# Two more landing buffers for weights, a mask added by matmul, and another order of first loads, in a fused attention and MoE kernel

## The chip, the cores and the metric

One core of one Trainium2 chip runs the whole program. The metric is the device time of one execution in microseconds (us); lower is better. The core has TensorE (PE in the rows; PEld is its weight load), VectorE (DVE), ScalarE (ACT) and GpSimd (POOL); SyncE (SP) issues most of the DMAs.

## The reference

Attention in windows, then two MoE-like blocks, all in fp32:

```python
scores = q @ k.T / sqrt(64)       # 4 batches, 8 heads, 576 positions
# heads 0-3: the last 32 positions; heads 4-7: every 4th of the last 128
attn = softmax(where(mask, scores, -1e9)); x = attn @ v        # 2304 x 512
y = ((x @ w1) * (x @ w2)) @ w3 @ w_out                         # 512 -> 1024 -> 512
z = (silu(y @ w_gate) * (y @ w_val)) @ moe2_w_out              # 512 -> 1536 -> 512
```

## The kernel before

**Numbers.** Every weight and activation that a large matmul uses is kept as a high and a low part, and each product is three matmuls into one bank (`mm3`, lines 182 to 187). The 37 weight blocks of 1 MB hold 64-bit words and are turned into parts on the chip (`convert_weights`, lines 152 to 173): a DMA lands the block in a `raw` buffer, ScalarE rescales the upper words (L166), VectorE shifts the lower words right by 29 (L167) and joins the two (L168), ScalarE copies the high part (L172), GpSimd subtracts for the low part (L173). Then the buffer is given back and the next load is issued (`done_with`, `load_block`). There are three `raw` buffers while blocks 0 to 19 pass, then two.

**Stages.** First, w3 and w_out of the first MoE block are multiplied into one matrix W in 16 steps s (lines 431 to 451). Steps 0 to 7 need one new block each among 0 to 7 (a pair of blocks per two steps from 2 on), steps 8 to 15 one per two steps (blocks 8 to 11). In between stand the units of attention of batch 0: its four pairs of heads, each in `scores`, `transposes` and `values`; they end in `x0`, the tokens of chunk 0. Blocks 12 to 19 are w1 and w2. Then `stage1` takes 5 chunks of 512 tokens (the last has 256) through w1, w2 and W, with the attention of batches 1 to 3 inside chunks 0 to 2; it goes through DRAM (`x1d`) into the next chunk's `x`. The second MoE block follows (lines 513 to 537).

**Scores** (lines 280 to 317): 5 or 4 matmuls per group fill a bank; VectorE scales and adds the mask (L300) and takes the row maximum (L303); ScalarE does 9 exponentials a pair (L305); VectorE adds 1e-9 and inverts (L308, L309); GpSimd multiplies (L310). The transposes (L323) go back through ScalarE (L325), the values are L338.

**Order.** Each engine runs its instructions in the order of its queue. A scheduler fixes that order when the program is built, from a model of durations.

Of the kernel before, what the change touches and what calls it, by code (L numbers as in the profile page):

```python
# [70 lines left out]
def moe_chain_kernel(tc, q_in, k_in, v_in, w_in, mask_in, out):  # L71
# [8 lines left out]
    with static as st, other as ot, psum as pp, dram as dp:  # L80

        wslot = [st.tile([P, 2, 2, 512], F32R, name=f"w{i}") for i in range(12)]
        xb = [st.tile([P, 2, KT, CMAX], F32R, name=f"x{i}") for i in range(2)]
# [154 lines left out]
        att1_pool = tc.tile_pool(name="att1", bufs=1)  # L238
        att2_pool = tc.tile_pool(name="att2", bufs=1, side="right")
        with att1_pool as a1, att2_pool as a2:  # L240
# [8 lines left out]
            sc = [a2.tile([P, NBLK, KW], F32, name=f"s{i}") for i in range(2)]  # L249
            pt = a2.tile([P, NBLK, P], F32, name="pt")  # L250
            mask = a2.tile([P, NBLK, KW], F32, name="mask")
            ident = a2.tile([P, P], F32, name="ident")
            sm = [a2.tile([P, 3, NBLK], F32, name=f"sm{i}") for i in range(2)]
# [26 lines left out]
            def scores(i, g):  # L280
# [11 lines left out]
                v = ps[:, :nb * KW].rearrange("p (n k) -> p n k", k=KW)  # L292
                if i % NPAIR >= NPAIR // 2:
                    parts = [(b0, b1, mask[:, b0:b1])]
                else:
                    parts = [(0, 1, mask[:, 0:1])] if g == 0 else []
                    lo = max(b0, 1)
                    parts.append((lo, b1, mask[:, 1:2].to_broadcast([P, b1 - lo, KW])))
                for lo, hi, mk in parts:
                    nc.vector.scalar_tensor_tensor(  # L300
# [303 lines left out]
```

## Time and profile before

| what | us |
|---|---|
| median of 3 runs (907.78 to 911.71) | 909.82 |
| the profiled execution, its own time | 909.69 |
| its span, first to last instruction | 907.5 |
| TensorE busy | 881.4 (97%) |
| VectorE, ScalarE, GpSimd busy | 336.0, 312.3, 132.0 |

TensorE's busy time counts pipelined matmuls from start to a modelled end, so 97% does not mean that it runs at its peak. The granted clock (PEclk) is a share of 2.4 GHz; 0.5 is the lower level, 1.2 GHz.

### The profile page before, as it was taken

The page shows a single profiled execution, that of the slowest core. Times are in us where ns is not written, and L with a number is a line of the kernel's source. Part 1 is how long each engine was busy: PE and PEld are TensorE (multiplying, and loading weights), DVE is VectorE, ACT ScalarE, POOL GpSimd, SP SyncE. Part 2 cuts the span into 40 slices and gives each one's busy share as a digit, 9 for nine tenths or more (in the row PEclk, how much of TensorE's full clock was granted, in tenths as well). Part 3 has the DMA queues.
Part 4 walks back from the last instruction along what each step waited for, and adds up shares of the span by engine and source line. Part 5 has one row for each costly group of instructions (what it writes and reads, how often), then busy time and mean ns, then how long its engine had stood idle before and what let it go on. Part 6 is the DMA issues. An engine that isn't in the chain of part 4 may idle for free.

```text
span 907.5 us, 11771 instructions
## 1 busy us (share of the span) xinstructions
PE 881.4 (97%) x4850; PEld 737.6 (81%) x4850; DVE 336.0 (37%) x487; ACT 312.3 (34%) x682; POOL 132.0 (15%) x83
## 2 busy tenths in 40 slices
PE   8889899989999999999999999999999999999998
PEld 5667688868888878889988888888888888888998
DVE  5887952333324213344766313111221112111221
ACT  4966743343525423343555212111221112111111
POOL 4656531000100100321343000000000000000000
PEclk8989899999999999999999999999999999999999
DMA  9786622332224113333555302000010001000100
GB/s 296 253 275 237 211 61 61 93 126 88 77 91 155 33 46 116 122 119 139 208 178 173 106 1 70 1 0 1 1 47 1 0 1 47 1 0 1 47 1 24
DMA packets 45909, 79.58 MB, mean 88 GB/s; under 512 B 3232, under 2 KB 29472, under 8 KB 41120
## 3 DMA queue, kind: packets, MB, share of 16 engines
q1 hardware_dynamic: 40096, 69.39, 23.5%
q10 hardware_dynamic: 5760, 9.44, 2.8%
q8 instruction: 38, 0.62, 0.3%
q14 instruction: 15, 0.12, 0.0%
HBM read 65.72 MB, written 13.11 MB: 87 GB/s over the span
## 4 chain that ended last, share of the span: by engine, by line
PE 83%; DVE 6%; DMA 4%; ACT 3%; issue 2%; POOL 1%; SPq 0%; DVEq 0%; POOLq 0%; ACTq 0%
PE bk L185 26%; PE bk L186 26%; PE bk L187 26%; PE bk L286 3%; DMA raw<-w_in 2%; DVE raw L168 2%; PE bk L338 2%; DVE raw L167 2%; PE bk L323 1%; POOL w L173 1%; ACT raw L166 1%; ACT s L305 1%; DMA q<-q_in 1%; ACT w L172 1%; DMA raw<-x1d 1%
## 5 line engine op out<-in xcount | busy, mean ns | idle before, releaser
L185 PE MATMUL bk<-x,w 128*128 128x512 f32 (+1 forms) x640 | 239.8, 375 | 3.2 <-ACT x L134 2.5
L186 PE MATMUL bk<-x,w 128*128 128x512 f32 (+1 forms) x640 | 238.5, 373 | 1.4 <-DVE x L135 1.4
L187 PE MATMUL bk<-x,w 128*128 128x512 f32 (+1 forms) x640 | 238.2, 372 | 0.0
L210 DVE TENSOR_TENSOR ta<-bk,ta 128x512 f32<-128x512 f32 (+1 forms) x100 | 63.7, 637 | 354.7 <-PE bk L187 323.7
L185 PEld LDWEIGHTS bk<-x,w 128*128 128x128 f32 x640 | 121.5, 190 | 23.5 <-ACT x L134 2.9
L186 PEld LDWEIGHTS bk<-x,w 128*128 128x128 f32 x640 | 121.6, 190 | 21.4 <-DVE x L135 2.4
L187 PEld LDWEIGHTS bk<-x,w 128*128 128x128 f32 x640 | 121.6, 190 | 19.8
L204 ACT ACTIVATE ta<-bk 128x512 f32<-128x512 f32 (+1 forms) x100 | 55.3, 553 | 227.2 <-PE bk L187 215.5
L186 PE MATMUL bk<-p,w 128*128 128x512 f32 (+1 forms) x320 | 118.5, 371 | 1.1 <-DVE p L135 1.1
L187 PE MATMUL bk<-p,w 128*128 128x512 f32 (+1 forms) x320 | 118.0, 370 | 0.0
L185 PE MATMUL bk<-p,w 128*128 128x512 f32 (+1 forms) x320 | 117.0, 371 | 0.0
L134 ACT ACTIVATE p<-ta 128x512 fp32r<-128x512 f32 (+1 forms) x100 | 58.7, 587 | 161.8 <-DVE ta L210 161.7
L135 DVE TENSOR_TENSOR p<-ta,p 128x512 fp32r<-128x512 f32 (+1 forms) x100 | 78.7, 787 | 55.3 <-ACT p L134 55.0
L173 POOL TENSOR_TENSOR w<-raw,w 128x1024 fp32r<-128x1024 f32 (+1 forms) x33 | 81.5, 2473 | 98.2 <-ACT w L172 98.2
L186 PEld LDWEIGHTS bk<-p,w 128*128 128x128 f32 x320 | 60.4, 189 | 11.6 <-DVE p L135 1.7
L187 PEld LDWEIGHTS bk<-p,w 128*128 128x128 f32 x320 | 60.4, 189 | 9.9
L185 PEld LDWEIGHTS bk<-p,w 128*128 128x128 f32 x320 | 59.8, 189 | 10.0 <-ACT p L134 0.2
L305 ACT ACTIVATE s<-s,sm 128x96 f32<-128x96 f32 x144 | 52.0, 363 | 41.3 <-DVE sm L303 41.2
L168 DVE SCALAR_TENSOR_TENSOR raw<-raw 128x1024 uint32<-128x1024 uint32 (+1 forms) x39 | 59.4, 1522 | 10.9 <-ACT raw L166 10.0
L310 POOL TENSOR_TENSOR s<-s,sm 128x480 f32<-128x480 f32 (+1 forms) x32 | 32.8, 1024 | 192.7 <-DVE sm L309 119.1
L166 ACT ACTIVATE raw<-raw 128x1024 f32<-128x1024 f32 (+1 forms) x39 | 43.8, 1124 | 30.1 <-DMA raw<-w_in 30.1
L172 ACT ACTIVATE w<-raw 128x1024 fp32r<-128x1024 f32 (+1 forms) x33 | 36.7, 1113 | 39.3 <-DVE raw L168 39.2
(80 smaller groups left out, 952.5 us busy)
## 6 DMA issues: line engine op xcount, KB each, us to landing
raw<-w_in SPq DMA_DIRECT2D x37, 1024.0 KB, 5.2
v<-v_in SPq DMA_DIRECT2D x16, 432.0 KB, 4.0
q<-q_in SPq DMA_DIRECT2D x32, 160.0 KB, 4.2
k<-k_in SPq DMA_DIRECT2D x16, 288.0 KB, 5.7
x2d<-o ACTq DMA_DIRECT2D x16, 256.0 KB, 2.0
raw<-x2d SPq DMA_DIRECT2D x4, 1024.0 KB, 5.2
out_t<-o ACTq DMA_DIRECT2D x16, 256.0 KB, 2.0
x1d<-o SPq DMA_DIRECT2D x12, 288.0 KB, 3.8
```

The lines of the kernel that those rows point to most:

```text
L134: nc.scalar.activation(hi, src, AF.Copy)
L135: return nc.vector.tensor_tensor(out=lo, in0=src, in1=hi.bitcast(F32), op=ALU.subtract)
L166: nc.scalar.activation(hi.bitcast(F32), hi.bitcast(F32), AF.Prelu, scale=REBIAS, alpha=SIGN_UP)
L168: nc.vector.scalar_tensor_tensor(out=lo, in0=hi, scalar=3, in1=lo, op0=ALU.logical_shift_left, op1=ALU.bitwise_or)
L172: nc.scalar.activation(w[:, :, 0], x, AF.Copy)
L173: nc.gpsimd.tensor_tensor(out=w[:, :, 1], in0=x, in1=w[:, :, 0].bitcast(F32), op=ALU.subtract)
L185: nc.tensor.matmul(ps, wh, xh, start=start, stop=False)
L186: nc.tensor.matmul(ps, wh, xl, start=False, stop=False)
L187: nc.tensor.matmul(ps, wl, xh, start=False, stop=stop)
L204: nc.scalar.activation(ta[:, :n], ba[:, :n], func)
L210: nc.vector.tensor_tensor(out=u, in0=bb[:, :n], in1=ta[:, :n], op=ALU.mult)
L305: nc.scalar.activation(s[:, n], s[:, n], AF.Exp, bias=m[:, 0, n:n + 1], accum_out=m[:, 1, n:n + 1])
```

## The change

- The second chunk buffer `x1` is no longer allocated from the start. Its room holds two more `raw` buffers (five in all) that are used for blocks below N_EARLY = 12; `second_x` makes `x1` out of that room at the end of chunk 0. The number of a buffer decides in `done_with` how long it is given back.
- The right shift by 29 becomes a multiplication and a subtraction on the same tile (L174 of the new program in place of L167).
- In batch 0 the mask is added on TensorE: a matmul of a bf16 identity with a bf16 mask opens the bank's sum (L315). The maximum is taken from the bank (L327), GpSimd scales it (L328), and the exponentials read the bank (L341). Two casts on GpSimd make the bf16 mask (L456, L463), one the identity (L451).
- In all batches the 1e-9 is added on GpSimd (L344 in place of L308).
- The first loads are mask, k, q of pair 0, then weights.

```diff
+N_EARLY = N_W1 - 8
...
+TOP3 = 2.0 ** -29 * (1 - 2.0 ** -16)
+DOWN = 0.5 - 7.5 * 2.0 ** -16
...
-        xb = [st.tile([P, 2, KT, CMAX], F32R, name=f"x{i}") for i in range(2)]
+        xb = [st.tile([P, 2, KT, CMAX], F32R, name="x0")]
...
         def done_with(n):
-            if n < N_W1 or raw_at[n] is not raw[2]:
+            here = [r is raw_at[n] for r in raw].index(True)
+            if here < 2 or n < (N_W1 if here == 2 else N_EARLY):
                 raw_free.append(raw_at[n])
             load_block()
...
                 nc.scalar.activation(hi.bitcast(F32), hi.bitcast(F32), AF.Prelu, scale=REBIAS, alpha=SIGN_UP)
-                nc.vector.tensor_scalar(out=lo, in0=lo, scalar1=29, scalar2=None, op0=ALU.logical_shift_right)
+                nc.vector.tensor_scalar(out=lo, in0=lo, scalar1=TOP3, scalar2=DOWN, op0=ALU.mult, op1=ALU.subtract)
...
+        def second_x():
+            early_pool.__exit__(None, None, None)
+            xb.append(late_pool.__enter__().tile([P, 2, KT, CMAX], F32R, name="x1"))
...
             raw.append(a1.tile([P, 2, 512, 2], U32, name="raw2"))
+            raw.extend(ep.tile([P, 2, 512, 2], U32, name=f"raw{i}") for i in (3, 4))
...
+                if i < NPAIR:
+                    for lo, hi in parts:
+                        nc.tensor.matmul(
+                            v[:, lo - b0:hi - b0], identb, masks(maskb, lo, hi), start=lo == b0, stop=False
+                        )
                 for n in range(b0, b1):
                     nc.tensor.matmul(
-                        ps[:, (n - b0) * KW:(n - b0 + 1) * KW],
+                        v[:, n - b0],
                         q[:, QB + 2 * QB * n:QB + 2 * QB * (n + 1)],
                         kk[:, n * QB:n * QB + KW],
-                        start=True, stop=True,
+                        start=i >= NPAIR, stop=i >= NPAIR or n == b1 - 1,
                     )
...
+                if i < NPAIR:
+
+                    nc.vector.tensor_reduce(out=m[:, 0, b0:b1], in_=v, op=ALU.max, axis=AX.X, negate=True)
+                    nc.gpsimd.tensor_scalar(
+                        out=m[:, 0, b0:b1], in0=m[:, 0, b0:b1], scalar1=scale, scalar2=None, op0=ALU.mult
+                    )
+                    src, by = v, scale
...
                 for n in range(b0, b1):
                     nc.scalar.activation(
-                        s[:, n], s[:, n], AF.Exp, bias=m[:, 0, n:n + 1], accum_out=m[:, 1, n:n + 1]
+                        s[:, n], src[:, n - b0], AF.Exp, bias=m[:, 0, n:n + 1], scale=by, accum_out=m[:, 1, n:n + 1]
                     )
-                nc.vector.tensor_scalar_add(m[:, 1, b0:b1], m[:, 1, b0:b1], 1e-9)
+                nc.gpsimd.tensor_scalar(
+                    out=m[:, 1, b0:b1], in0=m[:, 1, b0:b1], scalar1=1e-9, scalar2=None, op0=ALU.add
+                )
...
-            load_block()
+            nc.gpsimd.tensor_copy(identb, ident)
+            nc.sync.dma_start(out=mask[:, :2], in_=mask_in[:, :2])
             load_k(0)
             load_q(0)
-            nc.sync.dma_start(out=mask[:, :2], in_=mask_in[:, :2])
+            load_block()
+            nc.gpsimd.tensor_copy(maskb[:, :2], mask[:, :2])
+            load_v(0)
             load_block()
             load_k(1)
             load_q(1)
-            load_v(0)
             load_block()
             nc.sync.dma_start(out=mask[:, 2:], in_=mask_in[:, 2:])
+            nc.gpsimd.tensor_copy(maskb[:, 2:], mask[:, 2:])
+            load_block()
+            load_block()
...
                 if k == K1 - 1:
+                    if len(xb) == 1:
+                        second_x()
                     next_block()
```

SyncE's queue at the start of the program, where `raw` are weight blocks (in the change `raw_106` to `raw_108` are buffers 2 to 4). Before:

```order
L125 DMA raw_82<-w_in 128x1024 x2
L266 DMA k_104<-k_in 128x576
L263 DMA q_102<-q_in 64x5x128 x2
L416 DMA mask<-mask_in 128x192
L125 DMA raw_83<-w_in 128x2048
L266 DMA k_105<-k_in 128x576
L263 DMA q_103<-q_in 64x5x128 x2
L271 DMA v<-v_in 96x9x128
L125 DMA raw_107<-w_in 128x2048
L422 DMA mask<-mask_in 128x672
L263 DMA q_102<-q_in 64x5x128
```

With the change:

```order
L452 DMA mask<-mask_in 128x192
L284 DMA k_103<-k_in 128x576
L281 DMA q_101<-q_in 64x5x128 x2
L131 DMA raw_81<-w_in 128x1024 x2
L289 DMA v<-v_in 96x9x128
L131 DMA raw_82<-w_in 128x2048
L284 DMA k_104<-k_in 128x576
L281 DMA q_102<-q_in 64x5x128 x2
L131 DMA raw_106<-w_in 128x2048
L462 DMA mask<-mask_in 128x672
L131 DMA raw_107<-w_in 128x2048
L131 DMA raw_108<-w_in 128x2048
```

Mask, k and q of pair 0 now stand ahead of the first weight block, and five blocks are issued where three were, before the reload of q for pair 2.

VectorE, softmax of the first pair, before (`sm` holds maxima and sums, `bk` are PSUM banks):

```order
L300 SCALAR_TENSOR_TENSOR s_109<-bk_93,mask 128x96
L300 SCALAR_TENSOR_TENSOR s_109<-bk_93,mask 128x384
L303 TENSOR_REDUCE sm_114<-s_109 128x5
L300 SCALAR_TENSOR_TENSOR s_109<-bk_88,mask 128x384
L167 TENSOR_SCALAR raw_83<-raw_83 128x1024
L303 TENSOR_REDUCE sm_114<-s_109 128x4
L308 TENSOR_SCALAR sm_114<-sm_114 128x5
L309 RECIPROCAL sm_114<-sm_114 128x5
```

GpSimd at the same place with the change:

```order
L456 CAST maskb<-mask 128x192
masks.py:199 ISA
masks.py:199 AFFINE_SELECT ident<-ident 128x128
L451 CAST identb<-ident 128x128
L180 TENSOR_TENSOR w_66<-raw_81,w_66 128x512
L328 TENSOR_SCALAR sm_117<-sm_117 128x5
L328 TENSOR_SCALAR sm_117<-sm_117 128x4
L180 TENSOR_TENSOR w_66<-raw_81,w_66 128x512
L344 TENSOR_SCALAR sm_117<-sm_117 128x5
L348 TENSOR_TENSOR s_110<-s_110,sm_117 128x480
L344 TENSOR_SCALAR sm_117<-sm_117 128x4
L348 TENSOR_TENSOR s_110<-s_110,sm_117 128x384
```

VectorE's mask additions and its 1e-9 are gone there; GpSimd now has the casts, and the scale (L328) and the 1e-9 (L344) between subtractions (L180, before L173).

TensorE where chunk 0 ends and the first matmul on chunk 1's `x` stands (L185/L192 on `x_79`/`x_1393`). Before:

```order
L185 MATMUL bk_89<-p,w_77 128x512
L186 MATMUL bk_89<-p,w_77 128x512
L187 MATMUL bk_89<-p,w_77 128x512
L323 MATMUL bk_93<-ident,s_109 96x128 x3
L323 MATMUL bk_92<-ident,s_109 96x128 x3
L185 MATMUL bk_90<-x_79,w_69 128x512
```

With the change:

```order
L319 MATMUL bk_92<-k_104,q_102 128x96 x5
L319 MATMUL bk_91<-k_104,q_102 128x96 x4
L192 MATMUL bk_85<-p,w_77 128x512
L193 MATMUL bk_85<-p,w_77 128x512
L194 MATMUL bk_85<-p,w_77 128x512
L192 MATMUL bk_86<-p,w_77 128x512
L193 MATMUL bk_86<-p,w_77 128x512
L194 MATMUL bk_86<-p,w_77 128x512
L192 MATMUL bk_87<-p,w_77 128x512
L193 MATMUL bk_87<-p,w_77 128x512
L192 MATMUL bk_89<-x_1393,w_69 128x512
```

From the last `values` matmul of batch 1 to that first matmul there are 27 large matmuls, 9 of scores and 6 transposes before, and 43 large ones and 9 of scores with the change.

## Rows read from the trace of the kernel before

**Rows 1.** stretches: length, busy us of PE, PEld, DVE, ACT, POOL, granted clock, DMA share, GB/s
```profile
0.00:40.00 40.00, 32.26 (x215) 24.45 (x216) 26.57 (x44) 27.05 (x78) 19.08 (x24) 0.91 0.93 296
...
50.00:60.00 10.00, 6.91 (x54) 5.57 (x54) 8.84 (x11) 6.10 (x8) 6.04 (x4) 0.66 1.00 311
...
94.00:104.00 10.00, 6.76 (x25) 5.62 (x26) 9.55 (x12) 6.90 (x9) 5.26 (x2) 0.66 0.82 258
...
112.00:907.00 795.00, 786.81 (x4291) 662.83 (x4290) 247.15 (x372) 236.55 (x504) 69.50 (x42) 1.00 0.19 64
...
186.00:193.00 7.00, 4.68 (x12) 3.46 (x13) 3.31 (x5) 4.66 (x13) 1.81 (x2) 0.76 0.64 225
...
600.00:700.00 100.00, 100.00 (x441) 82.58 (x440) 20.77 (x29) 18.08 (x29) 0.00 (x0) 1.00 0.03 11
```

**Rows 2.** groups by line from 0 to 112 us: xcount | busy, mean ns | idle before
```profile
L185 PE MATMUL bk<-w,w 128*128 128x512 f32 x56 | 22.7, 423 | 2.0 <-ACT w L172 2.0
...
L185 PE MATMUL bk<-x,w 128*128 128x512 f32 x16 | 7.1, 446 | 1.3 <-DVE ta L210 0.7 <-ACT x L134 0.6
...
L286 PE MATMUL bk<-k,q 128*128 128x96 f32 x108 | 17.2, 316 | 4.8 <-DMA q<-q_in 2.6 <-DVE xr L369 2.3
...
L323 PE MATMUL bk<-ident,s 128*96 128x128 f32 x42 | 6.5, 274 | 1.6 <-DVE s L300 0.8 <-DVE x L135 0.4 <-POOL s L310 0.3
...
L338 PE MATMUL bk<-pt,v 96*64 96x64 f32 x136 | 5.7, 228 | 4.6 <-ACT pt L325 4.6
```

**Rows 3.** TensorE in order of time: start, us, what, xcount
```profile
16.88 2.15 PE L286 MATMUL bk<-k,q 128*128 128x96 f32 x18
...
41.54 1.03 PE L403 MATMUL bk<-ta 128*128 128x512 bf16 x4
...
51.07 1.39 PE L338 MATMUL bk<-pt,v 96*64 96x64 f32 x40 [1.18 <-ACT pt L325]
```

**Rows 4.** waits of SyncE's queue, 0 to 113 us: total, times, longest
```profile
SPq L125 <- POOL w L173: 44.6, 15, 7.3
```

**Rows 5.** weight block 7 in order of time: its load, its shift, its first matmul
```profile
42.75 1.12 SPq L125 DMA_DIRECT2D raw<-w_in  x1
...
49.09 2.75 DVE L167 TENSOR_SCALAR raw<-raw 128x1024 uint32<-128x1024 uint32 x1 [1.30 <-DMA raw<-w_in]
...
54.48 0.80 PE L185 MATMUL bk<-w,w 128*128 128x512 f32 x1 [2.02 <-ACT w L172]
```

**Rows 6.** conversion steps of VectorE and GpSimd in order of time, alone and side by side
```profile
27.50 0.69 DVE L167 TENSOR_SCALAR raw<-raw 128x1024 uint32<-128x1024 uint32 x1
...
59.34 2.85 POOL L173 TENSOR_TENSOR w<-raw,w 128x1024 fp32r<-128x1024 f32 x1 [2.41 <-ACT w L172]
...
60.37 2.92 DVE L168 SCALAR_TENSOR_TENSOR raw<-raw 128x1024 uint32<-128x1024 uint32 x1 [0.47 <-ACT raw L166]
```

**Rows 7.** groups by line from 7 to 57 us, GpSimd
```profile
L173 POOL TENSOR_TENSOR w<-raw,w 128x1024 fp32r<-128x1024 f32 (+1 forms) x9 | 20.4, 2280 | 12.7 <-ACT w L172 12.7
...
L310 POOL TENSOR_TENSOR s<-s,sm 128x480 f32<-128x480 f32 (+1 forms) x8 | 8.5, 1058 | 11.5 <-DVE sm L309 9.1 <-ACT w L172 2.4
```

**Rows 8.** groups by line from 7 to 57 us, VectorE
```profile
L308 DVE TENSOR_SCALAR sm<-sm 128x5 f32<-128x5 f32 (+1 forms) x8 | 3.5, 441 | 2.2 <-ACT s L305 2.1
```

**Rows 9.** DMA issues: count, KB each, median us from issue to landing
```profile
raw<-w_in SPq DMA_DIRECT2D x37, 1024.0 KB, 5.2
...
v<-v_in SPq DMA_DIRECT2D x16, 432.0 KB, 4.0
...
q<-q_in SPq DMA_DIRECT2D x32, 160.0 KB, 4.2
...
k<-k_in SPq DMA_DIRECT2D x16, 288.0 KB, 5.7
```

**Rows 10.** the change from token chunk 0 to 1, in order of time
```profile
176.90 0.67 DVE L363 COPY o<-bk 128x288 f32<-128x288 f32 x1 [6.96 <-PE bk L338]
...
186.69 1.06 ACT L134 ACTIVATE x<-raw 128x1024 fp32r<-128x1024 f32 x1 [1.13 <-DMA raw<-x1d]
```

More of the change, by code (lines that the diff above doesn't have):

```diff
@@ L236, in flush @@
                 pend.pop()()
-        att1_pool = tc.tile_pool(name="att1", bufs=1)
-        att2_pool = tc.tile_pool(name="att2", bufs=1, side="right")
-        with att1_pool as a1, att2_pool as a2:
+        early_pool = tc.tile_pool(name="early", bufs=1)
+        ep = early_pool.__enter__()
+        late_pool = tc.tile_pool(name="late", bufs=1, reuse_waits="tile")
+        def second_x():
+            early_pool.__exit__(None, None, None)
+            xb.append(late_pool.__enter__().tile([P, 2, KT, CMAX], F32R, name="x1"))
+        att_pool = tc.tile_pool(name="att", bufs=1, side="right")
+        with att_pool as a1:
             qd = [a1.tile([P, 2 * QB * (NBLK + 1)], F32, name=f"q{i}") for i in range(2)]
@@ L246, in moe_chain_kernel @@
             raw.append(a1.tile([P, 2, 512, 2], U32, name="raw2"))
+            raw.extend(ep.tile([P, 2, 512, 2], U32, name=f"raw{i}") for i in (3, 4))
             raw_free.extend(raw)
             xr = a1.tile([P, REST], F32, name="xr")
[L249 to L253, printed above, removed]
+            sc = [a1.tile([P, NBLK, KW], F32, name=f"s{i}") for i in range(2)]
+            pt = a1.tile([P, NBLK, P], F32, name="pt")
+            mask = a1.tile([P, NBLK, KW], F32, name="mask")
+            ident = a1.tile([P, P], F32, name="ident")
+            maskb = a1.tile([P, NBLK, KW], BF16, name="maskb")
+            identb = a1.tile([P, P], BF16, name="identb")
+            sm = [a1.tile([P, 3, NBLK], F32, name=f"sm{i}") for i in range(2)]
             def q_halves(q, j):
@@ L284, in scores, with masks @@
                 ps = att_bank()
+                dilated = i % NPAIR >= NPAIR // 2
+                v = ps[:, :nb * KW].rearrange("p (n k) -> p n k", k=KW)
+                if dilated:
+                    parts = [(b0, b1)]
+                else:
+                    parts = ([(0, 1)] if g == 0 else []) + [(max(b0, 1), b1)]
+                def masks(t, lo, hi):
+                    return t[:, lo:hi] if dilated or lo == 0 else t[:, 1:2].to_broadcast([P, hi - lo, KW])
+                if i < NPAIR:
[3 more added lines that the diff above has]
+                        )
@@ L293, in scores @@
-                if i % NPAIR >= NPAIR // 2:
-                    parts = [(b0, b1, mask[:, b0:b1])]
-                else:
[L296 to L300, printed above, removed]
-                        out=s[:, lo:hi], in0=v[:, lo - b0:hi - b0], scalar=scale, in1=mk, op0=ALU.mult, op1=ALU.add
-                    )
@@ L303, in scores @@
-                nc.vector.tensor_reduce(out=m[:, 0, b0:b1], in_=s[:, b0:b1], op=ALU.max, axis=AX.X, negate=True)
+                if i < NPAIR:
[4 more added lines that the diff above has]
+                    src, by = v, scale
+                else:
+                    for lo, hi in parts:
+                        nc.vector.scalar_tensor_tensor(
+                            out=s[:, lo:hi], in0=v[:, lo - b0:hi - b0], scalar=scale, in1=masks(mask, lo, hi),
+                            op0=ALU.mult, op1=ALU.add,
+                        )
+                    src, by = s[:, b0:b1], 1.0
+                    nc.vector.tensor_reduce(out=m[:, 0, b0:b1], in_=src, op=ALU.max, axis=AX.X, negate=True)
@@ L537, in moe_chain_kernel @@
             flush()
+        late_pool.__exit__(None, None, None)
 def mask_of():
```

2 lines of the change are left out of this document (1 added, 1 removed).

## The prediction

> **What bounds the kernel now.** I first read the stretches, to see where TensorE does not run at its pace. From 112 us to the end it is idle for 795 - 786.8 = 8.2 us, and in a dense stretch it starts 441 large matmuls in 100 us, 0.227 us each [rows 1]. Before 112 us it is different. The groups by line give 216 large matmuls there (72 on each of three lines), and steps 0 and 1 add 24, so 240 x 0.227 = 54.4 us; 108 score matmuls at 2.15 / 18 = 0.12, 42 transposes taken at the same, 136 value matmuls at 1.39 / 40 = 0.035 [rows 2, 3] make 12.9 + 5.0 + 4.7. That is 77 us of work in 112 us. So 35 us are lost before 112 us and some 8 after; only there can this change gain.
>
> Who is late in those 112 us? SyncE's queue waited 44.6 us for GpSimd's subtraction to give a buffer back before it could issue a weight load [rows 4]. Block 7 shows it: its load is issued at 42.75, VectorE had waited for it when it shifts at 49.09, and TensorE, idle for 2.0 us, starts on it at 54.48 [rows 5]. But loads are not alone. VectorE's shift takes 0.69 alone and 2.75 in block 7; the join (L168) that began at 60.37 ended at 63.29, just 1.10 after the subtraction that ran from 59.34 to 62.19 [rows 5, 6]. The two engines take turns. So two bounds lie close together: the loop of buffers, and the turns of VectorE and GpSimd.
>
> **The change, part by part.** The sum is made against the profiled execution, 909.69 us (span 907.5 and 2.2 around it), 0.1 below the median of the three runs.
>
> *Loads.* Up to block 7 the queue moves 8 blocks of 1024 KB, q and k of four pairs (4 x 608), v of two (864) and the masks (432): 11,920 KB or 12.2 MB [rows 9]. At the 296 GB/s of the first 40 us [rows 1], counted from 0, the last lands at 41.2, not at 49.1. If nothing else held it, TensorE would start on block 7 at 41.2 + (54.48 - 49.09) = 46.6, which is 7.9 us earlier. Mask, k and q moved ahead of block 0 put it behind 0.7 MB, 2.4 us later; that is inside the same total, and step 0 waits for it while the first scores run earlier. The two extra loads stand ahead of the reload of q and k for pair 2, which is needed after the softmax of two pairs: no cost taken.
>
> *Turns.* From 7 to 57 us, the time up to block 7's subtraction, GpSimd's subtractions hold 20.4 us and eight multiplications 8.5 [rows 7], and eight blocks x (0.69 + 1.10) of VectorE 14.3: 43.2 of 50 us, 86%. With the change two of the multiplications (pair 3) come later in GpSimd's queue, 6.4 remain; the casts of 992 columns cost between half of and the whole 2.45 ns a column that the multiplication needs for its two inputs [rows 7], 1.2 to 2.4, taken 1.5; twelve small operations that were VectorE's or new (scale and 1e-9) cost between next to nothing and the 0.44 that VectorE needed, waits included [rows 8], taken 0.2 each, 2.4. Sum 20.4 + 14.3 + 6.4 + 1.5 + 2.4 = 45.0. Without any gap block 7 is done at 52.0, at 86% at 59.3; in the profile at 56.9. With a block always waiting the gaps get fewer: I take 97%, 53.4, so **-3.5 us**. Bounds: -7.9 (loads alone) and +2.4 (86%).
>
> *The shift as arithmetic.* The row gives 0.69 us for 1024 columns [rows 6], which I keep for the new form, with its turn. The other bound is the join's 1.10, at one column at a time. The Trainium skill, "VectorE: DVE Perf Modes", section "The perf-mode tier table", has operations of a tensor with a scalar on 4-byte data in SBUF at two elements a cycle, arithmetic included; no run here shows the new form. By that the 0.69 stays; were the form slower but outside the turns, the ledger would fall by 8 x 0.69 = 5.5 to 39.5, block 7 would be done at 47.7 at the same 97%, and loads (49.0 for that step) would decide: 901 would become 898.
>
> *Softmax of batch 0.* VectorE loses 14 mask additions (L300) and eight 1e-9; in this stretch they are off the two bounds, but the mask additions stood before the exponentials. Against that the exponentials now wait for GpSimd (L328), behind whose subtraction everything that ScalarE has queued behind them waits too. In and out I count 0 here, and the bad case is a rival.
>
> *Mask matmuls.* Ten, with 3456 columns in all. Four of 512 bf16 columns take 1.03 us [rows 3], so 1.7 us at full clock, 3.5 at half. Most stand where TensorE waits anyway: **+0.5** (0 to +3.5). The banks are held until the exponentials have read them; the next writers of these banks stand 30 or more matmuls later in TensorE's order.
>
> *Clock.* In 50 to 60 us the granted clock is 0.66, so most of the stretch ran at the lower of the two levels, 1.2 GHz, after TensorE's idle time ahead of block 7 [rows 1, 5]. Its 6.9 busy us lose 2.3 us by that. A shorter wait may or may not keep the clock up: half, **-1.2** (0 to -2.3).
>
> *Stretch 94 to 104.* TensorE waits for the last pair's tokens: 3.2 us idle, and 6.8 at a clock of 0.66 [rows 1] lose 2.3 more. In the changed order the last pair's transposes and values stand behind the first 18 matmuls of chunk 0, so the same chain of copies is waited for: 0 (-5.5 at most).
>
> *From chunk 0 to 1.* The last values of batch 1 go through DRAM: VectorE's copy at 176.90, ScalarE on the reloaded tokens at 186.69 [rows 10]. Between stand 27 large matmuls, 9 of scores (18 rows) and 6 transposes, 6.1 + 2.1 + 0.7 = 9 us, and TensorE idles 7.0 - 4.7 = 2.3 us in 186 to 193, at a clock of 0.76 [rows 1], which costs 4.7 x 0.24 = 1.1 more. With the change 43 large ones and 9 of scores stand there, 9.8 + 2.1 = 11.9 us: 2.9 us more cover than before, more than the wait. It goes, with its clock: **-3.4**. At the next two chunk boundaries the cover is somewhat shorter than before: **+0.5** (0 to +2).
>
> *x1 made late* waits for the last user of buffers 3 and 4, blocks 8 to 12 or so, some 80 us before its first write: 0. *1e-9 on GpSimd in batches 1 to 3*: GpSimd has 69.5 busy us in the 795 after 112 [rows 1]: 0.
>
> Sum: -3.5 + 0.5 - 1.2 - 3.4 + 0.5 = -7.1, so **902.6 us**.
>
> **Rivals.**
>
> *The turns set the pace (R1).* The buffers bring nothing, since VectorE and GpSimd go on at 86%: block 7 is 2.4 us later, the clock gains nothing, the chunk boundary stays: +2.4 + 0.5 - 3.4 + 0.5 = 0, 909.7 us. For it: the 1.10 after the subtraction and the 2.75 for a shift of 0.69 [rows 5, 6]. Against it: GpSimd was idle 12.7 us before its subtractions in that stretch, waiting for ScalarE's copies [rows 7], and so for loads. The Trainium skill, "SBUF — State Buffer", section "Who interferes with whom", says that whichever of the two starts first keeps the shared ports for its whole instruction and the other fully blocks; the two rows of the join and the subtraction agree, 1.10 us of the join after the subtraction's end [rows 6].
>
> *Loads were the only bound (R2).* Then -7.9 for block 7, -2.3 of clock, and the wait in 94 to 104 goes too since blocks and tokens are ready (-5.5), + 0.5 - 4.3 (with no cost at later boundaries): 909.7 - 19.5 = 890.2 us.
>
> *GpSimd's hops (R3), slower.* Sixteen small operations of batch 0 now stand in GpSimd's queue between subtractions of 2.43 us, and ScalarE's whole queue, conversions included, stands behind the exponentials that wait for eight of them. Each that has to wait for a whole subtraction costs 2.43 us on the path. Three use up the gain; from five on the change is slower by over 0.5%. With six: 902.6 + 14.6 = 917.2 us. For it: GpSimd is busy for 19.1 of the first 40 us [rows 1], so about every second meets a subtraction. Against it: the order puts most of them between two subtractions, where ScalarE's next copy is waited for [rows 7], and the waits overlap with ScalarE's own work.
>
> **How the numbers follow.** A measurement of this kernel tells 0.5% (4.5 us) from no change, so faster means below 905.2, slower above 914.3. Forecast 0.55 (894 to 906 with its terms' bounds), R1 0.20, R2 0.17, R3 0.08. Faster: 0.55 x 0.93 + 0.17 + a tenth of R1 = 0.70; slower: R3 and 0.01 of R1 = 0.09; same 0.21. The range from 887 to 912 takes in the forecast, R2 and R1 and leaves out R3 and the tails, some 0.15.
>
> **What would show it.** SyncE's wait for GpSimd falls from 44.6 to under 20 us in the first 100 us; TensorE starts on block 7 at 50 to 52; the new shift takes 0.69 alone; TensorE's idle time before chunk 1 is under 1 us; the same work as at 112 us is done by about 108. R1 would show block 7 at 54 or later with short load waits; R2 a start at 47 and no wait for the last pair; R3 exponentials that wait for GpSimd by 10 us or more in total. I am wrong if TensorE's lost time before chunk 0's first matmuls does not fall, or if the gain after 112 us is missing.

## The result and the profile after

The change is slower: 918.01 us (917.19 to 919.27, four runs) against 909.41 (907.78 to 911.71), ratio 1.0094, 95% interval 1.0068 to 1.012. The forecast was 902.6 us, range 887 to 912. The profiled execution has a span of 915.8 us; the one before had 907.5, so 8.3 us have to be found.

One number tells where: TensorE's **lost time**, its idle time plus busy time x (1 - granted clock), added over stretches of 1 us (5 us behind 125). Of one profiled execution each, us:

| kernel | 0 to 85 | 85 to 125 | 125 to the end | sum |
|---|---|---|---|---|
| before | 17.6 | 8.5 | 10.3 | 36.4 |
| the change | 17.5 | 18.4 | 8.8 | 44.7 |

The sums differ by 8.3, as the spans do: 9.9 more in 85 to 125 us and 1.6 less elsewhere. How far such numbers can be trusted shows in `b_shift` (below), whose queues are those of the kernel before: its three columns differ from that kernel's by 0.9, 1.1 and 1.4 us. In long stretches (length, then busy us of PE, PEld, DVE, ACT, POOL, granted clock, DMA share, GB/s), before:

```profile
0.00:85.00 85.00, 73.21 (x438) 57.91 (x439) 64.58 (x88) 57.58 (x141) 48.55 (x36) 0.92 0.81 259
85.00:125.00 40.00, 34.38 (x215) 27.14 (x214) 32.84 (x37) 24.83 (x51) 20.16 (x10) 0.91 0.58 186
```

and with the change:

```profile
PE 884.7 (97%) x4860; PEld 739.3 (81%) x4860; DVE 323.1 (35%) x445; ACT 310.0 (34%) x682; POOL 151.4 (17%) x126
...
0.00:85.00 85.00, 72.62 (x425) 54.57 (x426) 58.94 (x60) 52.17 (x122) 64.47 (x54) 0.94 0.94 291
85.00:125.00 40.00, 30.04 (x157) 25.37 (x156) 26.81 (x38) 26.50 (x65) 19.80 (x14) 0.74 0.36 104
180.00:200.00 20.00, 20.00 (x131) 16.63 (x131) 7.55 (x12) 6.36 (x18) 0.00 (x0) 1.00 0.45 143
```

In 85 to 125 us TensorE is idle for 10.0 us (5.6 before), and its 30 busy us run at a clock of 0.74 (0.91). Up to 85 us nothing is won. From 180 to 200 it is busy throughout, where it waited before [rows 1, the stretch 186 to 193].

TensorE with the change, in order of time (start, us, what; in brackets the idle time before it and what ended it):

```profile
53.05 0.99 PE L192 MATMUL bk<-w,w 128*128 128x512 f32 x1
...
79.55 1.39 PE L376 MATMUL bk<-pt,v 96*64 96x64 f32 x40 [0.29 <-ACT pt L363]
...
89.72 4.15 PE L319 MATMUL bk<-k,q 128*128 128x96 f32 x18 [3.79 <-DVE xr L407]
...
104.08 0.87 PE L361 MATMUL bk<-ident,s 128*96 128x128 f32 x3 [3.41 <-ACT pt L363]
104.88 1.28 PE L376 MATMUL bk<-pt,v 96*64 96x64 f32 x20
106.90 1.34 PE L376 MATMUL bk<-pt,v 96*64 96x32 f32 x20 [0.74 <-ACT pt L363]
110.27 2.45 PE L319 MATMUL bk<-k,q 128*128 128x96 f32 x10 [2.03 <-DVE xr L407]
112.42 1.20 PE L192 MATMUL bk<-x,w 128*128 128x512 f32 x2
```

At 53.05 it starts on block 7 (54.48 before, [rows 5]). The values of pair 2 end at 80.94, but the scores that need their bank start only at 89.72: 3.79 us idle, and the 18 scores take 4.15 us where they took 2.15 [rows 3]. Then the transposes of pair 3 wait 3.41 us for ScalarE's copies (L363), and the first matmul on pair 3's tokens starts at 112.42, when the values have been done for 4.2 us.

VectorE and ScalarE in that stretch, with the change:

```profile
84.07 0.68 DVE L174 TENSOR_SCALAR raw<-raw 128x1024 uint32<-128x1024 uint32 x1
86.44 2.59 DVE L175 SCALAR_TENSOR_TENSOR raw<-raw 128x1024 uint32<-128x1024 uint32 x1 [1.70 <-ACT raw L173]
88.96 0.60 DVE L142 TENSOR_TENSOR x<-bk,x 128x256 fp32r<-128x256 f32 x1
89.47 0.20 DVE L407 COPY xr<-bk 128x32 f32<-128x32 f32 x1
...
106.51 3.06 DVE L175 SCALAR_TENSOR_TENSOR raw<-raw 128x1024 uint32<-128x1024 uint32 x1 [1.30 <-ACT raw L173]
109.50 0.60 DVE L142 TENSOR_TENSOR x<-bk,x 128x256 fp32r<-128x256 f32 x1
```

```profile
84.24 1.17 ACT L179 ACTIVATE w<-raw 128x1024 fp32r<-128x1024 f32 x1 [3.65 <-DVE raw L175]
85.30 1.12 ACT L173 ACTIVATE raw<-raw 128x1024 f32<-128x1024 f32 x1
86.31 1.08 ACT L141 ACTIVATE x<-bk 128x256 fp32r<-128x256 f32 x2
...
98.71 1.15 ACT L173 ACTIVATE raw<-raw 128x1024 f32<-128x1024 f32 x1 [1.11 <-DMA raw<-w_in]
99.77 0.36 ACT L341 ACTIVATE s<-s,sm 128x96 f32<-128x96 f32 x1
...
103.56 0.84 ACT L363 ACTIVATE pt<-bk 96x384 f32<-96x384 f32 x2
...
109.61 1.12 ACT L179 ACTIVATE w<-raw 128x1024 fp32r<-128x1024 f32 x1 [2.25 <-DVE raw L175]
110.63 0.61 ACT L141 ACTIVATE x<-bk 128x256 fp32r<-128x256 f32 x1
```

The copy that frees the bank (L142 at 88.96, L407) stands behind the join of block 15 (L175 at 86.44, 2.59 us), and ScalarE's half of the same tokens (L141 at 86.31) behind the high part of block 14 (L179, for which ScalarE waits 3.65 us on VectorE's join) and the rescaling of block 15 (L173). Block 15 (the joins counted from the start) holds w1 and w2 of the fourth eighth of chunk 0; the matmuls of three eighths stand ahead of its first use. Pair 3's copies (L363, 103.56) stand behind pair 4's exponentials (from 99.77), and these behind the rescaling of block 18, for which ScalarE waits 1.11 us on the load. At 106.51 a join of 3.06 us stands ahead of the tokens again, and ScalarE's next token copy (L141, 110.63) behind the high part of that block (L179).

In the kernel before, conversions stood ahead of pair 3's token copies too, but fewer. VectorE there:

```profile
91.75 2.71 DVE L168 SCALAR_TENSOR_TENSOR raw<-raw 128x1024 uint32<-128x1024 uint32 x1 [0.68 <-ACT raw L166]
...
94.99 0.60 DVE L135 TENSOR_TENSOR x<-bk,x 128x256 fp32r<-128x256 f32 x1
...
96.73 2.90 DVE L168 SCALAR_TENSOR_TENSOR raw<-raw 128x1024 uint32<-128x1024 uint32 x1 [0.45 <-ACT raw L166]
99.55 0.61 DVE L135 TENSOR_TENSOR x<-bk,x 128x256 fp32r<-128x256 f32 x1
```

These are the joins of blocks 15 and 16, and the last tokens are copied at 99.55. With the change the joins of 17, 18 and 19 stand ahead of them as well (94.52, 102.00 and 106.51), and they are copied at 111.27.

### The profile page after: what moved, and what is told of

Its sections match the earlier page's. It is cut to its first block, busy times and chain, and to the rows that moved or that the text cites. A ratio compares the mean times of both kernels' runs of the same rounds, so it can differ in the third digit from the quotient of the medians.

```text
span 915.8 us, 11772 instructions
## 1 busy us (share of the span) xinstructions
PE 884.7 (97%) x4860; PEld 739.3 (81%) x4860; DVE 323.1 (35%) x445; ACT 310.0 (34%) x682; POOL 151.4 (17%) x126
## 4 chain that ended last, share of the span: by engine, by line
PE 80%; DVE 5%; ACT 4%; DMA 2%; issue 2%; POOL 1%; ACTq 0%; DVEq 0%; POOLq 0%; SPq 0%
PE bk L192 25%; PE bk L193 25%; PE bk L194 25%; PE bk L319 2%; DVE raw L175 2%; PE bk L376 2%; PE bk L361 1%; ACT w L179 1%; ACT raw L173 1%; DVE raw L174 1%; DMA x2d<-o 1%; ACT s L341 1%; DVE p L142 1%; DMA raw<-x1d 1%; DMA raw<-w_in 1%
## 5 line engine op out<-in xcount | busy, mean ns | idle before, releaser
L192 PE MATMUL bk<-x,w 128*128 128x512 f32 (+1 forms) x640 | 237.7, 372 | 2.8 <-ACT ta L211 2.8
L192 PEld LDWEIGHTS bk<-x,w 128*128 128x128 f32 x640 | 121.1, 190 | 23.0 <-ACT ta L211 3.5
L141 ACT ACTIVATE p<-ta 128x512 fp32r<-128x512 f32 (+1 forms) x100 | 58.8, 588 | 181.2 <-DVE ta L217 181.1
L192 PE MATMUL bk<-p,w 128*128 128x512 f32 (+1 forms) x320 | 117.3, 371 | 0.0
L142 DVE TENSOR_TENSOR p<-ta,p 128x512 fp32r<-128x512 f32 (+1 forms) x100 | 76.1, 761 | 57.4 <-ACT p L141 57.4
L180 POOL TENSOR_TENSOR w<-raw,w 128x1024 fp32r<-128x1024 f32 (+1 forms) x33 | 82.0, 2491 | 85.1 <-ACT w L179 76.9
L175 DVE SCALAR_TENSOR_TENSOR raw<-raw 128x1024 uint32<-128x1024 uint32 (+1 forms) x39 | 64.6, 1655 | 13.1 <-ACT raw L173 12.3
L192 PEld LDWEIGHTS bk<-p,w 128*128 128x128 f32 x320 | 59.8, 189 | 9.8
L173 ACT ACTIVATE raw<-raw 128x1024 f32<-128x1024 f32 (+1 forms) x39 | 43.9, 1132 | 26.4 <-DMA raw<-w_in 26.4
L341 ACT ACTIVATE s<-s,sm 128x96 f32<-128x96 f32 x108 | 39.0, 362 | 36.1 <-DVE sm L339 36.1
L179 ACT ACTIVATE w<-raw 128x1024 fp32r<-128x1024 f32 (+1 forms) x33 | 37.2, 1126 | 40.7 <-DVE raw L175 40.6
L319 PEld LDWEIGHTS bk<-k,q 128*128 128x128 f32 x288 | 38.9, 209 | 10.1 <-DVE xr L407 6.4
```

The costliest lines, as they stand in the source:

```text
L141: nc.scalar.activation(hi, src, AF.Copy)
L142: return nc.vector.tensor_tensor(out=lo, in0=src, in1=hi.bitcast(F32), op=ALU.subtract)
L173: nc.scalar.activation(hi.bitcast(F32), hi.bitcast(F32), AF.Prelu, scale=REBIAS, alpha=SIGN_UP)
L175: nc.vector.scalar_tensor_tensor(out=lo, in0=hi, scalar=3, in1=lo, op0=ALU.logical_shift_left, op1=ALU.bitwise_or)
L180: nc.gpsimd.tensor_tensor(out=w[:, :, 1], in0=x, in1=w[:, :, 0].bitcast(F32), op=ALU.subtract)
L192: nc.tensor.matmul(ps, wh, xh, start=start, stop=False)
```

## The experiments

Each time is the median of 4 to 12 executions, in 5 rounds beside the kernel before, whose own median was 910.5 to 911.5 us from set to set; across sets, go by the ratios. Lost time is of one profiled execution, as above. The runs with a name in `a_`, `h1_after`, `due15`, `best15_6`, `best16_6` and `a3_due15g` start from the changed program, those in `b_`, `d_late` and `r5best15` from the kernel before.

| kernel | median us | ratio to before, interval | 0 to 85 | 85 to 125 | later |
|---|---|---|---|---|---|
| a_raw3 | 909.91 | 0.9995 (0.9979 to 1.0010) | 21.0 | 5.6 | 7.0 |
| b_raw5 | 911.85 | 1.0010 (0.9996 to 1.0024) | 21.4 | 11.0 | 7.3 |
| a_mask | 916.58 | 1.0066 (1.0047 to 1.0085) | 20.4 | 13.7 | 9.2 |
| a_units | 922.20 | 1.0118 (1.0097 to 1.0138) | 15.8 | 15.7 | 12.7 |
| d_late | 909.59 | 0.9983 (0.9967 to 0.9999) | 18.6 | 12.3 | 6.6 |
| h1_after | 915.66 | 1.0059 (1.0036 to 1.0083) | 23.8 | 6.0 | 10.1 |
| b_shift | 911.11 | 0.9998 (0.9983 to 1.0012) | 16.7 | 9.6 | 8.9 |
| b_loads | 912.64 | 1.0020 (1.0004 to 1.0035) | 21.5 | 10.9 | 8.1 |
| b_mask | 914.13 | 1.0027 (1.0012 to 1.0041) | 19.2 | 10.3 | 8.1 |
| b_raw5l | 916.82 | 1.0049 (1.0032 to 1.0066) | 21.4 | 13.2 | 8.2 |
| a_loads | 925.78 | 1.0148 (1.0126 to 1.0171) | 25.0 | 15.2 | 9.4 |
| due15 | 912.57 | 1.0013 (0.9996 to 1.0030) | 16.2 | 5.3 | 14.1 |
| best15_6 | 904.45 | 0.9921 (0.9905 to 0.9938) | 17.7 | 5.2 | 7.0 |
| best16_6 | 913.01 | 1.0019 (1.0004 to 1.0035) | 18.0 | 13.6 | 6.4 |
| b_gate | 907.70 | 0.9946 (0.9929 to 0.9963) | 16.5 | 9.9 | 6.4 |
| r5best15 | 907.29 | 0.9946 (0.9926 to 0.9966) | 21.3 | 1.6 | 7.9 |
| b_due15g | 903.98 | 0.9924 (0.9904 to 0.9943) | 16.4 | 7.2 | 7.0 |
| a3_due15g | 908.95 | 0.9975 (0.9960 to 0.9991) | 20.4 | 6.0 | 6.9 |

### First: which part, and is it TensorE's order?

The three theories are stated with the first run. Cover means the matmuls that stand in TensorE's order between some values and the first matmul that needs them.

**a_raw3**

```diff
-            raw_free.extend(raw)
+            raw_free.extend(raw[:3])
```

> The changed program with three weight buffers in use instead of five (the other two are made and left empty); all else of the change stays. Theory A (the two extra buffers let the order put weight steps earlier and the last pair's transposes and values of batch 0 behind chunk 0's first 18 matmuls): pair 3's values stand ahead of chunk 0 again, the 11 us lost between 85 and 118 us come back, 905 to 911 us. Theory B (the exponentials that read the bank hold the two attention banks, so attention runs one pair late): still 914 to 920. Theory C (VectorE and GpSimd take turns, and a conversion that never pauses pushes the tokens' small copies back): also 905 to 911, but then the changed order of the units in a_units does not help.

**b_raw5**: the change's lines on `raw3`, `raw4`, `done_with` and `second_x` put into the kernel before.

> The kernel before with five weight buffers and x1 made late as the only part of the change (shift, masks, 1e-9 and first loads as before). Theory A: slower than before, 913 to 921 us, with TensorE waiting in 85 to 118 us for pair 3's tokens. Theory B: faster than before, 901 to 907. Theory C: slower, 912 to 920, with little difference in the waits for the tokens' copies from the changed program.

**a_mask** (both places; the bf16 tiles go too)

```diff
-                if i < NPAIR:
+                if False:
```

> The changed program with batch 0's mask back on VectorE (no mask matmuls, no scale on GpSimd, the exponentials read and write the tile in SBUF); five buffers stay. Theory A: 913 to 919 us, less 1.5 at most for the matmuls. Theory B: the banks come free sooner and the loss goes: 901 to 909. Theory C: 910 to 917, since GpSimd has a few small operations fewer.

**a_units**

```diff
+                nxt = [(scores, i + 1, g) for g in range(2)] if i + 1 < NP else []
+                if i != NPAIR - 1:
+                    units += nxt
                 units += [(transposes, i, g) for g in range(3)]
                 units += [(values, i, g) for g in range(2)]
                 done_at.append(len(units))
+                if i == NPAIR - 1:
+                    units += nxt
```

> The changed program with the scores of batch 1's first pair written behind the transposes and values of batch 0's last pair instead of ahead of them; nothing else differs. Theory A: the wait for the bank (3.8 us) and the 3.4 us in which ScalarE does pair 4's exponentials before it copies pair 3's transposes go, with part of the low clock: 908 to 913 us. Theory B: 914 to 919, since the banks are still held. Theory C: 915 to 919, since conversion is as dense as before.

With three buffers the rest of the change is level with the kernel before (a_raw3), so the loss needs the buffers; alone they cost nothing that can be told (b_raw5: 911.85, just under what theory C had, with 2.5 us more lost in 85 to 125 us than before). Theory B is out as the main cause: without the mask matmuls 0.66% stays. Theory A failed on a_units, which is no faster than the change (1.0118 against 1.0094); its 922.2 lies above the ranges of B and C too. Two more runs tried TensorE's order from both sides.

**d_late** (`w_last` is the last matmul of step 15)

```diff
-                attend(min(2 * s + 4, done_at[1]))
-            attend(done_at[1])
+                attend(min(2 * s + 4, done_at[1] - 5))
+            with tc.issue_after(w_last[0].ins):
+                attend(done_at[1])
```

> The kernel before (three buffers, no part of the change) with one edit: the transposes and values of pair 3 of batch 0 are queued on TensorE behind the last matmul of step 15. In TensorE's order the values then end 0.4 us of matmuls ahead of the first matmul on pair 3's tokens, as in the changed program (0.6), where they end 6.7 us ahead in the kernel before. Theory A (this cover is what was lost): TensorE waits in 90 to 118 us for the tokens' copies, 5 to 9 us are lost there, and the later chunk boundaries, whose order moves too, give back 2 to 4: 911 to 917 us. Theory C (dense conversion): no change in that stretch, 905 to 909 us.

**h1_after** (`last_att` holds the last matmul of the units emitted so far)

```diff
+                    u = last_att.get(2 * (s - 1) + 4) if s >= 2 else None
+                    with tc.issue_after(u.ins) if u is not None else nullcontext():
-                    mm3(banks[kk], (w3[:, 0, c], w3[:, 1, c]), (wo[:, 0], wo[:, 1]), j == 0, j == K1 - 1)
+                        mm3(banks[kk], (w3[:, 0, c], w3[:, 1, c]), (wo[:, 0], wo[:, 1]), j == 0, j == K1 - 1)
```

> The changed program, whole, with each weight step queued on TensorE behind the attention units that the program text has emitted one step earlier. Pair 3's values then end 5.5 us of matmuls ahead of the first matmul on its tokens instead of 0.6. Theory A: most of the 9.3 us come back, 908 to 913 us. Theory C: conversion stays as dense, 915 to 919. If the weight steps themselves now wait for attention, it is slower than 919, and the wait must show on steps 9 to 15.

The late values cost 3.8 us in 85 to 125 (12.3 against 8.5), less than theory A had and more than the nothing of theory C, and the chunk boundary gave them back. In h1_after the loss moved ahead of 85 us instead of going (23.8 + 6.0). So the place in TensorE's order is a part at most: something delivers pairs 2 and 3 late wherever TensorE waits for them.

The other parts, alone or undone:

**b_shift**: L174 in place of L167, nothing else.

> The kernel before with the shift as multiplication and subtraction as its only edit; the order of every engine's queue is the same. My forecast: 0.69 us alone as before, taking turns with GpSimd as before, no change: within 0.2% of 909.8. If the new form is free of the turns: up to 3 us faster.

**b_loads**: the first loads of the change in the kernel before.

> The kernel before with the new order of the first loads as its only edit (three buffers, mask on VectorE). The order moves the later pairs as well: pair 3's values end 5.6 us of matmuls ahead of the first matmul on its tokens (6.7 before). Theory A: within 3 us of before, 906 to 911, as the cover is nearly kept. Theory C: the same. If the order of loads is itself part of the loss (916.6 of a_mask against 911.9 of b_raw5, which differ in it, the shift and the 1e-9): 912 to 916.

**b_mask**: the mask matmuls, GpSimd's scale and the exponentials from the bank in the kernel before.

> The kernel before with the mask matmuls of batch 0, GpSimd's scale and the exponentials from the bank as the only part of the change; three buffers, old loads, old shift, 1e-9 on VectorE. The new order of loads alone costs some 4 us before 85 us (b_loads), and a_raw3, which has it, ends level with before: without it 904 to 908 us. If the mask matmuls bring nothing by themselves: 909 to 912.

**b_raw5l**: buffers and first loads in the kernel before.

> The kernel before with two parts of the change: five buffers and the new order of first loads (each alone costs 0.1 to 0.2%). If the two together are what makes the change slow: 914 to 918 us. If the 1e-9 on GpSimd (all that a_mask has beside these two and the shift) has a part in it: 911 to 914.

**a_loads**: the change with the old first loads.

> The changed program with the first loads in the old order, five buffers. If buffers and loads together are the cause: 909 to 913 us, with less lost before 85 us. If buffers with the mask matmuls are: 915 to 919.

The shift costs nothing that can be told. The first loads alone cost 3.9 us up to 85 us, and TensorE shows a part of it: in b_loads its first step waits 5.93 us for block 0, where it waited 2.58 us for q, ahead of the first scores, in the kernel before. TensorE in the kernel before, then in b_loads:

```profile
9.03 4.13 PE L286 MATMUL bk<-k,q 128*128 128x96 f32 x18 [2.58 <-DMA q<-q_in]
12.86 0.77 PE L185 MATMUL bk<-w 128*128 128x512 f32 x1
...
15.56 0.80 PE L192 MATMUL bk<-w 128*128 128x512 f32 x1 [5.93 <-ACT w L179]
```

I had expected b_mask faster or level; it is slower by 0.27%. Buffers and loads together (b_raw5l) are as slow as a_mask, so the 1e-9 has no part in it that can be told. And the old loads under the rest of the change are the slowest of all (a_loads), against both expectations: it loses 7.5 us more than the change up to 85 us, where TensorE waits 6.2 us for ScalarE's copies of the transposes (0.3 with the change). The parts don't add up; each gives another order in every queue.

### Second: conversions that are not due

**due15**

```diff
-                while n_split[0] < min(s // 2 * 2 + 4, N_W1) and free:
+                while n_split[0] < min(s // 2 * 2 + 4, N_W1 if at[0] >= done_at[1] else 15) and free:
-                    next_block()
+                    next_block_late()
...
+        def next_block_late():
+            if n_split[0] < 15:
+                next_block()
+                return
+            with tc.issue_after(last_x[0].ins):
+                next_block()
```

> The changed program, whole, with VectorE's steps of weight blocks 15 to 19 (not needed before the fourth eighth of chunk 0) queued behind the last copy of batch 0's tokens on VectorE; TensorE's order is the same up to the first matmul on pair 3's tokens. Theory C in a sharper form (five buffers let conversions that are not due yet run ahead of the tokens that are): the 18.4 us that TensorE loses between 85 and 125 us fall to 9 to 13, 909 to 913 us in all. Theory A (TensorE's order alone): no change, 916 to 919. If blocks 15 to 19 then come too late themselves: new waits for ScalarE's weight copies after 115 us and no gain.

`last_x` is the last copy of batch 0's tokens on VectorE, and `issue_after` ties two instructions in the queue of that engine; the scheduler then moved some of ScalarE's and VectorE's other instructions too. TensorE's order up to the first matmul on pair 3's tokens differs by a few places only. The time is as expected, and 13.1 of the 18.4 us go, more than expected. VectorE, then TensorE, in due15:

```profile
80.94 3.26 DVE L175 SCALAR_TENSOR_TENSOR raw<-raw 128x1024 uint32<-128x1024 uint32 x1
86.99 0.62 DVE L142 TENSOR_TENSOR x<-bk,x 128x256 fp32r<-128x256 f32 x1 [2.79 <-ACT x L141]
87.52 0.20 DVE L416 COPY xr<-bk 128x32 f32<-128x32 f32 x1
```

```profile
87.78 3.24 PE L328 MATMUL bk<-k,q 128*128 128x96 f32 x18 [1.99 <-DVE xr L416]
...
96.34 0.81 PE L370 MATMUL bk<-ident,s 128*96 128x128 f32 x6
...
97.87 1.45 PE L385 MATMUL bk<-pt,v 96*64 96x64 f32 x40
100.13 1.35 PE L328 MATMUL bk<-k,q 128*128 128x96 f32 x10 [0.82 <-DVE xr L416]
...
180.00:200.00 20.00, 14.68 (x89) 11.11 (x89) 7.04 (x12) 8.72 (x28) 2.28 (x4) 0.83 0.46 151
```

No conversion stands ahead of the copy at 86.99 on VectorE now. It still waits 2.79 us for ScalarE's half of the tokens, so it comes only 2.0 us earlier. More is gained on ScalarE: block 18 is rescaled at 113.94 there, no longer ahead of pair 4's exponentials (98.71 with the change); these start at 93.12 (99.77), and pair 3's values at 97.87 instead of 104.88. But the last row shows a new loss of some 7 us at the change from chunk 0 to 1. It had two possible causes, the cover in TensorE's order or the late conversion.

**best15_6** (on top of due15; the seventh gate, `gate_a` at k = 6, is the product with the seventh eighth of w1), and **best16_6** with 16 in place of 15

```diff
+                    with tc.issue_after(pe_last[0].ins) if c == 0 and k == 6 and at[0] >= done_at[c + 2] else nullcontext():
-                    gate_a(("w1", k), x, n, AF.Copy)
+                        gate_a(("w1", k), x, n, AF.Copy)
```

> due15 with one more edit: in chunk 0 the seventh gate's matmuls are queued on TensorE behind the last values matmul of batch 1, so that 12.7 us of matmuls stand between those values and chunk 1's first matmul (6.1 in due15, 7.9 before, 10.8 with the change). If the loss of due15 at 185 to 195 us (7.1 us) is a matter of this cover: it falls to 0 to 2, 904 to 908 us in all, below the kernel before. If blocks 15 to 19, converted late, are what is waited for there: still 909 to 913.

> The same with blocks 16 to 19 instead of 15 to 19 behind the tokens' copies. Sharper theory C: one more conversion ahead of the tokens, 2 to 4 us more lost in 85 to 125 us than with 15 to 19, 906 to 911. If the number doesn't matter, the same as best15_6.

**b_gate**: the same edit on the kernel before.

> The kernel before (three buffers, nothing of the change) with only the seventh gate of chunk 0 queued behind batch 1's last values: 12.7 us of matmuls stand between them and chunk 1 where 7.9 stood. The 4.1 us lost in 185 to 195 us should go, as my forecast had it for the change: 905 to 908 us. If the tokens' way through DRAM gets longer with it, no change.

**r5best15**: five buffers alone, with both edits.

> The kernel before with five buffers alone (911.9 us, 11.0 us lost in 85 to 125 us) and the two queue edits of best15_6. If conversions that are not due are the cause with the buffers alone too: the 11.0 fall to 4 to 7, 903 to 908 us. If the cause belongs to the mask matmuls: 909 to 912.

It was the cover: the later loss falls from 14.1 to 7.0, and best15_6 takes 904.45 us, below both kernels. b_gate and r5best15 fall in their ranges too, and in r5best15 the 11.0 fall further than expected, to 1.6. best16_6 loses more than twice what I expected, 8.4 us more in 85 to 125 and 8.6 us in the median. Against best15_6 it has block 15's two steps on VectorE some twenty places earlier. ScalarE's order differs too: the high part of block 15 and the rescaling of block 18 stand ahead of pair 4's exponentials (block 18 is rescaled at 98.79, in best15_6 at 118.98). Beside that one copy on VectorE and a few matmuls stand in other places. Its trace shows both halves of the mechanism, VectorE

```profile
87.12 2.57 DVE L176 SCALAR_TENSOR_TENSOR raw<-raw 128x1024 uint32<-128x1024 uint32 x1 [1.71 <-ACT raw L174]
89.61 0.60 DVE L143 TENSOR_TENSOR x<-bk,x 128x256 fp32r<-128x256 f32 x1
```

and ScalarE, ahead of pair 4's exponentials and pair 3's copies (L375):

```profile
98.79 1.14 ACT L174 ACTIVATE raw<-raw 128x1024 f32<-128x1024 f32 x1 [3.18 <-DMA raw<-w_in]
99.82 0.38 ACT L353 ACTIVATE s<-s,sm 128x96 f32<-128x96 f32 x1
...
103.04 0.86 ACT L375 ACTIVATE pt<-bk 96x384 f32<-96x384 f32 x2
```

The join of block 15 takes 2.57 us ahead of the bank's copy, and ScalarE waits 3.18 us for block 18's load, with what TensorE needs queued behind it. In best15_6 the copy starts at 87.42, 2.2 us earlier, and the first exponential of pair 4 at 93.53, 6.3 us earlier:

```profile
87.42 0.63 DVE L143 TENSOR_TENSOR x<-bk,x 128x256 fp32r<-128x256 f32 x1 [2.76 <-ACT x L142]
...
93.53 0.37 ACT L353 ACTIVATE s<-s,sm 128x96 f32<-128x96 f32 x1
...
97.25 0.87 ACT L375 ACTIVATE pt<-bk 96x384 f32<-96x384 f32 x2 [0.40 <-PE bk L373]
```

So the 8.4 us are the price of block 15's place on VectorE together with what it drew along on ScalarE; no run parts the two.

Last, what the buffers are worth once the queues are mended: **b_due15g** is the kernel before, **a3_due15g** the change with three buffers in use, both with the two edits.

> The kernel before with three buffers and the two queue edits of best15_6 (VectorE's steps of blocks 15 to 19 behind the tokens' copies, the seventh gate behind batch 1's values); against r5best15 (907.3 us) it differs in the buffers alone. If two more buffers bring the 3.5 us that I forecast once the conversions wait their turn: 909 to 912 us. If they bring nothing: 905 to 908.

> best15_6 (904.5 us) with three buffers in use instead of five; all else of the change and both queue edits stay. If the two buffers bring 3.5 us: 907 to 910 us. If they bring nothing: 903 to 906.

Three buffers with nothing of the change, 903.98 us, come below both ranges and are level with best15_6 (ratios 0.9924 and 0.9921). So the gain of best15_6 over the kernel before is that of the two edits; the change adds nothing to it. On the kernel before the gate's edit alone has most of that gain (b_gate, 0.9946), and its interval overlaps with that of both edits: there the conversions' edit brings nothing that can be told. Within the change it does (due15, 1.0013 against 1.0094). Of the buffers alone: within the change with both edits they bring 4.5 us (908.95 to 904.45, intervals apart); without the rest of it no difference can be told (903.98 and 907.29, intervals overlap).

## Why the prediction was wrong

The forecast was -7.1 us and the spans gave +8.3. Of the 15.4 us between them 9.9 lie in 85 to 125 us, where I had put 0; 4.1 lie ahead of it (forecast -4.2 with the mask matmuls, measured -0.1), and 1.4 behind it (-2.9, measured -1.5).

**Loads and turns (-3.5) and clock (-1.2).** Up to 85 us nothing came: 17.6 and 17.5 us lost. TensorE started on block 7 at 53.05 (forecast 50 to 52), and SyncE's wait for GpSimd fell to 36.6 us, not below 20:

```profile
SPq L131 <- POOL w L180: 36.6, 11, 6.2
```

The term rested on "With a block always waiting the gaps get fewer", 97% for 86%, and that failed. GpSimd's idle time ahead of its subtractions in 7 to 57 us fell from 12.7 [rows 7] to 10.5 us only:

```profile
L180 POOL TENSOR_TENSOR w<-raw,w 128x1024 fp32r<-128x1024 f32 (+1 forms) x9 | 21.2, 2365 | 10.5 <-ACT w L179 10.5
```

A block was not always waiting: VectorE still waits for loads, 2.15 and 2.12 us ahead of its shifts at 15.34 and 23.88.

Within the change the buffers do bring something: three lose 21.0 us up to 85 (a_raw3), five 17.5. Of these 3.5 us, 1.3 are clock and 2.2 idle time, where I had summed 1.2 and 3.5. But a_raw3 has lost 3.4 more by then than the kernel before, by the other parts. "Inside the same total" failed for the first loads alone: the bytes are the same, but step 0 waits for block 0, and 3.9 us more are lost up to 85 (b_loads). For the change itself that isn't shown: its step 0 starts at 13.47, 0.6 us later than before, and with the old loads it loses more, not less (a_loads, 25.0). The mask matmuls alone lose 1.6 more there (b_mask), little above the 0.9 of b_shift. So which part takes back what the buffers bring stays open. It is no fixed gain of a buffer either, since alone they lose 3.8 more up to 85 (b_raw5). The clock's part of the loss up to 85 us fell from 5.8 to 5.1.

**Stretch 94 to 104 (0).** This step failed by most. I saw in the changed order that pair 3's transposes and values stand behind chunk 0's first matmuls, and said that "the same chain of copies is waited for". The chain's length isn't fixed: it is what stands ahead of each copy on VectorE and ScalarE, and I had read the changed order of TensorE, GpSimd and SyncE there, not that of these two. With more blocks at hand, joins of blocks 15 to 19 stand ahead of pair 3's last tokens, where those of 15 and 16 stood, and one of them ahead of pair 2's; on ScalarE the rescaling of block 18 stands ahead of pair 4's exponentials and so of pair 3's copies. 85 to 125 us cost 9.9 us more; due15 takes 13.1 of its 18.4 away, and putting block 15 back ahead of the tokens (best16_6 against best15_6), with block 18's rescaling drawn along, costs 8.4.

**Mask matmuls (+0.5) and softmax (0).** Ten matmuls, 2.7 us busy. Alone the part costs 2.5 us (0.27% of 909.4, b_mask), inside its range of 0 to +3.5.

**Shift.** 0.69 alone and in turns with GpSimd, as I kept it; ratio 0.9998 (b_shift). The changed program shows it alone and beside the subtractions:

```profile
51.81 0.68 DVE L174 TENSOR_SCALAR raw<-raw 128x1024 uint32<-128x1024 uint32 x1
...
77.82 2.93 DVE L174 TENSOR_SCALAR raw<-raw 128x1024 uint32<-128x1024 uint32 x1
```

The Trainium skill, "VectorE: DVE Perf Modes", section "The perf-mode tier table", has operations of a tensor with a scalar on 4-byte data in SBUF, arithmetic included, at two elements a cycle; the 0.68 of multiplication and subtraction, where the logical shift took 0.69 [rows 6], agrees.

**From chunk 0 to 1 (-3.4).** Right: some 4 us lost in 185 to 195 before, 1.2 in 200 to 205 now, and b_gate, which changes this cover alone, is 3.8 us faster (907.70 against 911.46). **Later boundaries (+0.5):** 1.6 us at 285, in the range.

**Rivals.** R1 was right that the first part brings nothing, but not by its reason: its sign, block 7 at 54 or later, did not come (53.05), and its 909.7 was wrong. R2's start at 47 did not come either. R3's 917.2 is near the result by accident: its sign was to be 10 us of exponentials waiting for GpSimd, and there are 2.48 and 0.81, ahead of 85 us, where no more is lost than before. No rival named VectorE's and ScalarE's queues at chunk 0's start.

**Sums.** R2 counts the chunk boundary at -4.3 where the term is -3.4, which would give 891.1. The shift's "901 would become 898" starts from 902.6. The join takes 1.21 by itself, not the 1.10 read from where it ended, so the ledger's 14.3 would be 15.2. The bounds of the terms, all added, reach from 890.6 to 914.2 and not from 894 to 906. None of this moves the forecast by more than 1 us.

**Open.** Why the parts don't add up (a_loads, b_raw5l) was not traced further; each gives another order in every queue. How the loss in 85 to 125 us divides between VectorE's and ScalarE's queue was not tested. Conversions of blocks below 15 behind the tokens weren't tried.

## What to carry to other kernels

A buffer that lets work start earlier also lets work that is not due stand ahead of work that is, in queues that run in order: before adding buffers, look in the new order for what stands ahead of each short copy on the path, on every engine of the chain, not only on the engine that waits. Then mend that with an order edge and time the edge alone: here two edges on the unchanged kernel gave all of the gain (0.9924), and the gate's edge alone most of it (0.9946). And count, at each place where results become inputs, how much independent work stands between: the term for that, -3.4, held.
